# One 384-column f32 product for signal and taps, and one strided product for both masks of a score piece

## The chip, the core and the metric

The kernel runs on one core of a Trainium2 chip. The metric is the device time of one execution in microseconds, as the median of several runs; smaller is better. Five engines work beside each other on the core, each in its own fixed order and tied to the others by semaphores: TensorE (PE in the profile, its weight loads PEld), VectorE (DVE), ScalarE (ACT), GpSimd (POOL) and SyncE (SP), which issues most transfers here.

## The reference

Two independent blocks are computed, and their outputs stand side by side in the last axis.

```python
# A: sliding-window attention, S = 2048, D = 576, H = 32 heads of 18, window 256
qkv = (x @ wqkv).reshape(B, S, 3, H, Dh) ...
scores = einsum("bhqd,bhkd->bhqk", q, k) * Dh ** -0.5
mask = (i - j >= 0) & (i - j < 256)
o = softmax(where(mask, scores, -1e9)) @ v
a = o.reshape(B, S, D) @ wo
# B: S4 convolution, L = 2048, D = 576, N = 128 states
K[d, l] = Re sum_n C[d, n] * exp(dt[d] * A[d, n] * l) * dt[d] * B[d, n]
b = irfft(rfft(pad(u)) * rfft(pad(K)))[:L] + u * Dskip
return concatenate([a, b], axis=-1)
```

## The kernel before, in words

The convolution is a two-step Fourier transform. In the first half of the program the signal and the taps K go through a first transform step and are stored in DRAM as `gx` (signal) and `gk` (taps); the projections for q, k and v are made there too. The second half, stage "rest" of the plan, mixes the attention with the rest of the convolution. This stage is what the change touches.

**Spectra.** The second transform step is done in 24 executions (3 groups of 192 channels by 8 groups of frequencies). `conv_load(n)` (line 655) loads one tile `tx` [128, 4, 192] of the signal and one tile `tk` of the taps by two transfers of the SP queue (line 660); `cload` lets execution n be loaded once the products of n - 2 are issued. `spectra(n)` (line 665) then takes two slots of PSUM, `px` for the signal and `pk` for the taps, and does 16 f32 products into each (line 675): for i (real or imaginary result), q, s, r one product with 64 rows, 32 columns of weights and 192 columns of data. The 16 weight pieces are the same for signal and taps. Each f32 product appears in the trace as two matmul instructions and two weight loads. Three later steps follow: `first` copies the signal's spectrum `px` into SBUF as X on ACT (line 684); `second` multiplies X by the real and by the imaginary part of `pk` on DVE (lines 690 and 691); `third` makes the two sums on POOL (lines 696, 697) into Y. `inverse` (line 708) takes Y back by one step in one slot, with a copy on ACT (line 715), and `clast` (line 769) does the last step.

**Slots.** `slot()` (line 180) takes one tile [128, 2, 512] f32 of the pool `ring`, which has three such slots of two PSUM banks each. A slot can be written again when its last reader is done. Nearly all products of stage "rest" write to this ring: spectra two slots at a time, and one slot each for the inverse step, the last step, the row maxima (`smax1`, products at line 836, masks at line 844, DVE maxima at line 870), the transpose of the maxima (line 852), the scores and the output projection (line 178). Only P times V (line 956) has its own PSUM tile `po`.

**Scores.** For each of 16 sets (4 query chunks by 4 head groups) there are five pieces by two halves `pp`, 160 score pieces in all. `score1` (line 910) takes a slot, does four products for each key block of the piece (line 921), and then adds the mask as further products: the identity times a table `tm` that holds 0 or a very large negative number (line 930). `masks` lists the blocks of 64 columns in which a mask stands and joins neighbours to a run of 64 or 128 columns. Four of the five pieces have two such runs, apart from each other, the fifth has one; each run is four products of 64 rows by 64 columns of weights (two banks b by two row halves r, which lie on four different quarters of the array). So a set does 2 x 36 mask products. ACT then takes the exponential of the piece into P (line 936).

**Order.** Each engine works in the order in which the program issues its instructions, and this order is written out as a string of letters, `PLAN` (line 85): a letter is the next step of a stream (c spectra, a scores, s maxima, v P times V, d inverse, e last step, k loads of the convolution), and a letter with a digit is a posted later step of that stream (c1 is `first`, c2 `second`, c3 `third`; a1 is the exponential). The string is the same before and after the change.

Of the kernel before, what the change touches and what calls it, by code (L numbers as in the profile page):

```python
# [10 lines left out]
F32 = mybir.dt.float32  # L11
# [31 lines left out]
def constants():  # L43
    c = {}
    tau = 2 * np.pi
    l1, l2, f1, f2 = np.arange(64), np.arange(32), np.arange(64), np.arange(32)
    ph = -tau * np.outer(l1, f1 + 0.25) / 64
    m = np.stack([np.cos(ph), np.sin(ph)], 2).reshape(64, 128)
    wu = np.concatenate([m, m])
    wk = np.tile(m.reshape(32, 2, 128), (4, 1, 1))  # L50
    w2 = np.zeros((2, 2, 32, 8, 2, 2, 64))
    i1 = np.zeros((4, 32, 8, 2, 2, 64))
    for f in range(64):
        t, s, b = f // 8, f // 4 % 2, f % 4
# [12 lines left out]
    for nm, v in mult.items():  # L67
        t = np.zeros((3, GC, GC, len(v)))
        for g in range(GC):
            t[:, g, g] = v  # L70
        c[nm] = t.reshape(96, GC, len(v))
    big = -3e38
    p, x = np.arange(64)[:, None], np.arange(64)[None]
    sm = np.concatenate([np.where(x <= p, big, 0), np.where(x > p, big, 0)], 1)
    far, near, no = np.where(x >= p, big, 0), np.where(p > x, big, 0), np.zeros((64, 64))
    tm = np.concatenate([far, near, near, far, far, no], 1)
    c["c_sm"], c["c_tm"] = np.concatenate([sm, sm]), np.concatenate([tm, tm])
    c["c_if"] = np.eye(128)
# [52 lines left out]
class Kernel:  # L131
# [522 lines left out]

    def conv_load(self, n):
        nc, fs, (ch, t) = self.nc, self.p["fs"], divmod(n, 8)
        r = []
        for nm, g in (("tx", self.gx), ("tk", self.gk)):
            x = fs.tile([128, 4, 192], F32, name=nm)
            nc.sync.dma_start(x, g[8 * t:8 * t + 8, :, :, 192 * ch:192 * ch + 192]  # L660
                              .rearrange("(s r) a l j -> (r a l) s j", r=2))
            r.append(x)
        self.cl[n] = r

    def spectra(self, n):
        nc, tt, fy, t = self.nc, self.nc.vector.tensor_tensor, self.p["fy"], n % 8
        px, pk = self.slot(), self.slot()
        for x, ps in zip(self.cl.pop(n), (px, pk)):
            for i in range(2):
                for q in range(2):  # L670
                    for s in range(2):
                        for r in range(2):
                            b = 2 * q + (r ^ s)
                            o = (2 * s + q) * 64 + 32 * i
                            nc.tensor.matmul(ps[32 * b:32 * b + 32, s, 192 * i:192 * i + 192],  # L675
                                             self.w2[64 * r:64 * r + 64, t, o:o + 32],
                                             x[64 * r:64 * r + 64, 2 * s + q],
                                             start=(i == 0), stop=True, skip_group_check=True)
        v = lambda z: z[:, :, :384].rearrange("p s (i j) -> p s i j", i=2)
        sh = [128, 2, 2, 192]  # L680

        def first():
            X = fy.tile(sh, F32, name="X")
            nc.scalar.activation(X, v(px), AF.Copy)
            self.post("2", (X, pk), lambda: second(X))

        def second(X):
            t1 = fy.tile(sh, F32, name="t1")
            t2 = fy.tile(sh, F32, name="t2")
            tt(t1, X, v(pk)[:, :, 0:1].to_broadcast(sh), op=OP.mult)  # L690
            tt(t2, X, v(pk)[:, :, 1:2].to_broadcast(sh), op=OP.mult)  # L691
            self.post("3", (t1, t2), lambda: third(t1, t2))

        def third(t1, t2):
            Y = self.Y[n] = self.p["fs"].tile(sh, F32, name="Y")
            nc.gpsimd.tensor_tensor(Y[:, 0], t1[:, :, 0], t2[:, :, 1], op=OP.subtract)  # L696
            nc.gpsimd.tensor_tensor(Y[:, 1], t1[:, :, 1], t2[:, :, 0], op=OP.add)
            self.n["Y"] += 1
        self.post("1", (px, pk), first)

    def inverse(self, n):
        nc, (ch, t), Y = self.nc, divmod(n, 8), self.Y.pop(n)
# [36 lines left out]
    def cspec(self):  # L739
        self.spd = set()  # L740
        for n in range(24):
            yield "PE", lambda: self.cl[n], "ring", "ring", lambda: n in self.cl and self.n["Y"] >= n
            self.spectra(n)
            self.spd.add(n)

# [38 lines left out]
    def att_setup(self):  # L784
        nc, a, ap = self.nc, self.a, self.p["att"]
        self.idb = ap.tile([128, 64], BF, name="idb")
        self.sm = ap.tile([128, 128], BF, name="sm")
        self.tm = ap.tile([128, 384], BF, name="tm")
        self.idf = ap.tile([128, 128], F32, name="idf")
        for t, n in ((self.idb, "c_id"), (self.sm, "c_sm"), (self.tm, "c_tm"), (self.idf, "c_if")):  # L790
            nc.sync.dma_start(t, a[n])
        self.sets = []
        for b in range(3):
            d = {"Q": ap.tile([128, 4, CQ], F16, name="Q%d" % b), "K": ap.tile([128, 4, CK], F16, name="K%d" % b),
                 "V": ap.tile([128, 12 * 76 + 16], F32, name="V%d" % b)}
# [73 lines left out]
    def red(self, out, x):  # L869
# [2 lines left out]

    TB = [[(-1, 0), (4, 256)], [(-3, 0), (0, 128), (-4, 448)], [(7, 0), (1, 64), (6, 384)], [(-2, 0), (2, 192)],
          [(3, 0), (5, 320)]]
    MO = {(0,): 0, (1,): 64, (0, 1): 0, (1, 0): 128, (0, 0): 192, (1, 1): 64}

    def blocks(self, n, c):
        r = []
# [3 lines left out]
                r.append((rel, o, q0, q1 - q0))  # L882
        return r

    def masks(self, bl):
        m = {}
        for rel, o, q0, w in bl:
            if rel >= 0:
                m[o // 64] = 1
            if rel <= 3:  # L890
                m[(o + w) // 64 - 1] = 0
        ms, r = sorted(m.items()), []
        while ms:
            e = ms.pop(0)
            if ms and ms[0][0] == e[0] + 1:
                r.append((e[0], (e[1], ms.pop(0)[1])))
            else:
                r.append((e[0], (e[1],)))
        return r

    def scores(self):
        for i in range(16):
            for n in (2, 4, 0, 1, 3):
                bl = self.blocks(n, i // 4)
                self.Ps[i, n] = P = []
                for pp in range(2):
                    yield "PE", (self.sets[i % 3]["Q"],), "ring", lambda: self.maxed > i and len(self.Ps) < 3
                    self.score1(bl, self.sets[i % 3], pp, P)

    def score1(self, bl, d, pp, Ps):  # L910
        nc = self.nc
        ps = self.slot()
        lo = min(x[1] for x in bl)
# [1 line left out]
        for k, (rel, off, q0, w) in enumerate(bl):  # L915
            for b in range(2):
                for r in range(2):
# [3 lines left out]
                    nc.tensor.matmul(ps[z:z + 64, b, off:off + w], d["K"][rr, 2 * b + pp, kc:kc + 64],  # L921
                                     d["Q"][rr, 2 * b + pp, q0:q0 + w], start=(k == 0), stop=False,
                                     skip_group_check=True)
        for blk, kinds in self.masks(bl):
            w = 64 * len(kinds)
            for b in range(2):
                for r in range(2):
                    z = 64 * (r ^ b)
                    rr = slice(64 * r, 64 * r + 64)
                    nc.tensor.matmul(ps[z:z + 64, b, 64 * blk:64 * blk + w], self.idb[rr],  # L930
                                     self.tm[rr, self.MO[kinds]:self.MO[kinds] + w], start=False, stop=True,
                                     skip_group_check=True)

        def go():
            P = self.p["P"].tile([128, 2, 512], F32, name="P")
# [267 lines left out]
```

## Time and profile before

| | |
|---|---|
| median of 3 runs | 883.02 us (873.43 to 885.18) |
| profiled execution, its own time | 884.13 us |
| its span, first to last instruction | 882.3 us |
| mean granted TensorE clock | 0.922 |
| PE busy over the span | 724.2 us, 82% |
| DVE, ACT, POOL busy | 599.7, 522.7 and 378.0 us |

The profile comes from one execution and has several views: the page with busy times and costliest groups; the groups of instructions by line and shape (busy time together, mean ns of one, idle time before them and what ended it); the waits (who waited for whom: us in total, times, longest); the table by stretches; the timeline (start, length, engine, line, operation, output and inputs, shape, count). "Issue" as the end of a wait means that the trace shows nothing the engine waited for. A row such as "64*32 64x192 f32" is a product with 64 rows, 32 weight columns and 192 data columns. A matmul's end is modelled, so products on different parts of the array overlap in the rows, and the distance between starts says more than the length.

### The profile page before, as it was taken

What the parts mean: (1) busy time and instruction counts of PE and PEld (TensorE: products, weight loads), DVE (VectorE), ACT (ScalarE), POOL (GpSimd) and SP (SyncE); (2) the same over time, 40 slices, a digit from 0 to 9 for tenths busy, and PEclk for the clock granted to TensorE, in tenths of its full rate; (3) what the DMA queues carried; (4) which work ended last, traced back from release to release, by engine and by line L of the source; (5) the groups of instructions that cost most, each with busy time, mean ns of one, the idle gap of its engine ahead of it and who ended that gap; (6) DMA issues with size and microseconds to landing.
All of it is one profiled execution on the core that took longest, in us unless ns stands there. A gap on an engine that the chain in (4) does not pass through costs nothing.

```text
span 882.3 us, 32024 instructions
## 1 busy us (share of the span) xinstructions
PE 724.2 (82%) x14234; PEld 440.0 (50%) x14234; DVE 599.7 (68%) x798; ACT 522.7 (59%) x685; POOL 378.0 (43%) x295
## 2 busy tenths in 40 slices
PE   4565957998889789886888888887998987999977
PEld 2321523456446545454555554455555554567655
DVE  5855887887987787768657796575876767861010
ACT  3247676678777857671455566555766666676421
POOL 2256867766687655665015142221332042432020
PEclk9885969999999999996889999869999999999998
DMA  9795261546247745458549667637639573846743
GB/s 310 256 230 137 61 160 34 141 100 175 63 106 199 152 116 161 99 158 233 145 147 293 212 212 232 163 103 240 204 120 270 166 227 116 264 144 181 236 143 129
DMA packets 211051, 150.85 MB, mean 171 GB/s; under 512 B 102698, under 2 KB 191530, under 8 KB 210656
## 3 DMA queue, kind: packets, MB, share of 16 engines
q1 hardware_dynamic: 208896, 144.80, 58.5%
q0 software_dynamic: 2016, 3.99, 1.5%
q8 instruction: 112, 1.84, 0.9%
q14 instruction: 27, 0.22, 0.1%
HBM read 83.50 MB, written 65.11 MB: 168 GB/s over the span
## 4 chain that ended last, share of the span: by engine, by line
PE 46%; DVE 17%; ACT 12%; issue 10%; DMA 6%; SPq 4%; POOL 4%; ACTq 0%; DVEq 0%; POOLq 0%
PE pp L178 9%; PE po L956 7%; PE ring L178 6%; DVE m L870 5%; ACT P L936 4%; PE ring L708 4%; PE ring L921 4%; PE ring L836 3%; PE ring L675 3%; PE ring L575 2%; PE ring L453 2%; PE ring L769 2%; PE ring L465 2%; DMA K<-kz 1%; DVE m L552 1%
## 5 line engine op out<-in xcount | busy, mean ns | idle before, releaser
L870 DVE TENSOR_REDUCE m<-ring 128x2 f32<-128x640 f32 (+4 forms) x256 | 187.7, 779 | 66.6 <-PE ring L844 61.5
L936 ACT ACTIVATE P<-ring,esc 128x1024 f32<-128x1024 f32 (+2 forms) x160 | 166.8, 1060 | 102.3 <-PE ring L930 91.7
L546 POOL TENSOR_TENSOR m<-A,tr 128x1024 f32<-128x1024 f32 x72 | 144.0, 2017 | 79.2 <-DVE m L552 66.7
L956 PE MATMUL po<-P,V 64*32 64x320 f32 (+4 forms) x2816 | 105.7, 369 | 6.3 <-issue 6.3
L836 PE MATMUL ring<-K,Q 54*64 54x320 f16 (+4 forms) x1024 | 82.3, 322 | 26.5 <-DMA K<-kz 8.6
L696 POOL TENSOR_TENSOR Y<-t,t 128x384 f32<-128x384 f32 x24 | 24.0, 998 | 139.2 <-DVE t L691 133.3
L990 POOL TENSOR_TENSOR osb<-osb,T 128x1024 f32<-128x1024 f32 x16 | 37.8, 2362 | 100.6 <-DVE T L985 80.9
L921 PE MATMUL ring<-Q,K 55*64 55x320 f16 (+4 forms) x1408 | 67.7, 270 | 14.1 <-ACT P L936 3.4
L836 PEld LDWEIGHTS <-Q 54*64 54x64 f16 x1024 | 42.8, 109 | 71.7 <-issue 63.4
L998 POOL TENSOR_TENSOR oh<-osb,oh 128x1024 f16<-128x1024 f32 x16 | 34.1, 2130 | 73.5 <-ACT oh L994 73.5
L178 PE MATMUL pp<-xh,wh 128*128 128x512 f16 x180 | 48.6, 401 | 19.0 <-ACT vst L365 9.6
L178 PEld LDWEIGHTS <-wh 128*128 128x128 f16 x324 | 31.7, 101 | 57.1 <-issue 17.6
L844 PE MATMUL ring<-sm,idb 64*64 64x128 bf16 x896 | 56.9, 229 | 1.5 <-issue 1.5
L552 DVE TENSOR_TENSOR m<-m,m 128x1024 f32<-128x1024 f32 x36 | 53.3, 1480 | 4.8 <-POOL m L546 4.7
L956 PEld LDWEIGHTS po<-P,V 64*32 64x32 f32 x2816 | 39.1, 108 | 34.5 <-issue 25.0
L575 PE MATMUL ring<-Q,m 128*32 128x64 f32 x2304 | 42.6, 231 | 16.1 <-DVE m L552 13.4
L921 PEld LDWEIGHTS <-K 55*64 55x64 f16 x1408 | 33.8, 110 | 42.7 <-issue 34.0
L575 PEld LDWEIGHTS ring<-Q,m 128*32 128x32 f32 x2304 | 37.0, 117 | 29.8 <-issue 12.6
L178 PE MATMUL pp<-xh,wl 128*128 128x512 f16 x180 | 49.9, 412 | 0.0
L981 DVE STREAM_TRANSPOSE T<-osb 128x1024 f32<-128x1024 f32 x16 | 19.8, 1235 | 42.7 <-ACT osb L966 42.7
L930 PE MATMUL ring<-tm,idb 64*64 64x128 bf16 (+1 forms) x1152 | 44.9, 213 | 2.9 <-issue 2.9
L527 POOL TENSOR_TENSOR tr<-tr,mab 128x768 f32<-128x768 f32 x18 | 33.6, 1867 | 31.2 <-ACT tr L522 31.1
(162 smaller groups left out, 1570.2 us busy)
## 6 DMA issues: line engine op xcount, KB each, us to landing
gx<-ust SPq DMA_DIRECT2D x16, 576.0 KB
gk<-kst SPq DMA_DIRECT2D x18, 512.0 KB
tx<-gx SPq DMA_DIRECT2D x24, 384.0 KB
tk<-gk SPq DMA_DIRECT2D x24, 384.0 KB
h<-ho SPq DMA_DIRECT2D x48, 192.0 KB
hp<-h SPq DMA_DIRECT2D x12, 768.0 KB
Q<-qz SPq DMA_DIRECT2D x16, 512.0 KB
K<-kz SPq DMA_DIRECT2D x16, 512.0 KB
```

What stands on the lines that cost most here:

```text
L178: self.nc.tensor.matmul(ps, u, v, start=(i == 0), stop=(i == len(ops) - 1))
L546: tt(m[part], A[:, ch, a0:a0 + 8].unsqueeze(3).to_broadcast(sh), tr[:, ch, part, 0:8].unsqueeze(2).to_broadcast(sh), op=OP.mult)
L552: self.nc.vector.tensor_tensor(m[0], m[0], m[1], op=OP.add)
L575: nc.tensor.matmul(kp[32 * st:32 * st + 32, j, :], m[:, ch, 32 * term:32 * term + 32], Q[:, ch, term, :], start=(term == 0), stop=(term == ...
L836: nc.tensor.matmul(ps[z:z + 64, b, :n], d["Q"][rr, 2 * b + pp, 64 * qb:64 * qb + 64], d["K"][rr, 2 * b + pp, k0:k1], start=True, stop=Fals ...
L844: nc.tensor.matmul(out, self.idb[rr], self.sm[rr], start=False, stop=True, skip_group_check=True)
L870: self.nc.vector.tensor_reduce(out, x, axis=AX.X, op=OP.max)
L921: nc.tensor.matmul(ps[z:z + 64, b, off:off + w], d["K"][rr, 2 * b + pp, kc:kc + 64], d["Q"][rr, 2 * b + pp, q0:q0 + w], start=(k == 0), st ...
L930: nc.tensor.matmul(ps[z:z + 64, b, 64 * blk:64 * blk + w], self.idb[rr], self.tm[rr, self.MO[kinds]:self.MO[kinds] + w], start=False, stop ...
L936: nc.scalar.activation(P[:, :, lo:hi], ps[:, :, lo:hi], AF.Exp, scale=self.esc)
L956: nc.tensor.matmul(po[32 * p:32 * p + 32, z, q0:q0 + w], V[64 * z:64 * z + 64, kb * 76 + 19 * p:kb * 76 + 19 * p + 32], P[p % 2][64 * z:64 ...
L990: nc.gpsimd.tensor_tensor(osb, osb, rb, op=OP.mult)
```

## The change

Two things change, and the order of steps does not.

Spectra: signal and taps come into one tile `xk` [128, 4, 2, 192], by the same two transfers. One product takes the 2 x 192 = 384 columns of both for each weight piece, so there are 16 f32 products instead of 32. The two slots now hold the results by i instead of by signal and taps: `pi[i]` has the signal's spectrum in columns 0 to 191 and that of the taps in columns 192 to 383 of each bank. The copy X becomes two ACT instructions, one out of each slot, and each of the two DVE products reads the taps out of one slot.

Masks: the two runs of a piece are made in one product whose output has two runs, a fixed number of blocks apart. `MS` (sets 4 to 15) and `MF` (sets 0 to 3, which have no keys before them) give for each piece the place in the table, the first block, the width of a run and the step between the runs (0 for one run). Runs of unequal width are widened to 128 columns, with zeros (`no`) or where the table has what is needed. The table `tm` grows from 384 to 640 columns. A set now does 2 x 20 mask products.

```diff
-    tm = np.concatenate([far, near, near, far, far, no], 1)
+    tm = np.concatenate([near, near, far, near, far, far, near, no, far, near], 1)
...
-        r = []
-        for nm, g in (("tx", self.gx), ("tk", self.gk)):
-            x = fs.tile([128, 4, 192], F32, name=nm)
-            nc.sync.dma_start(x, g[8 * t:8 * t + 8, :, :, 192 * ch:192 * ch + 192]
+        x = self.cl[n] = fs.tile([128, 4, 2, 192], F32, name="xk")
+        for m, g in enumerate((self.gx, self.gk)):
+            nc.sync.dma_start(x[:, :, m], g[8 * t:8 * t + 8, :, :, 192 * ch:192 * ch + 192]
                               .rearrange("(s r) a l j -> (r a l) s j", r=2))
...
+        x, pi = self.cl.pop(n), (self.slot(), self.slot())
+        for i in range(2):
+            for q in range(2):
+                for s in range(2):
+                    for r in range(2):
+                        b = 2 * q + (r ^ s)
+                        o = (2 * s + q) * 64 + 32 * i
+                        nc.tensor.matmul(pi[i][32 * b:32 * b + 32, s, :384], self.w2[64 * r:64 * r + 64, t, o:o + 32],
+                                         x[64 * r:64 * r + 64, 2 * s + q].rearrange("p m j -> p (m j)"),
+                                         start=True, stop=True, skip_group_check=True)
...
-            nc.scalar.activation(X, v(px), AF.Copy)
-            self.post("2", (X, pk), lambda: second(X))
+            for i in range(2):
+                nc.scalar.activation(X[:, :, i], pi[i][:, :, :192], AF.Copy)
+            self.post("2", (X, *pi), lambda: second(X))
...
-            tt(t1, X, v(pk)[:, :, 0:1].to_broadcast(sh), op=OP.mult)
-            tt(t2, X, v(pk)[:, :, 1:2].to_broadcast(sh), op=OP.mult)
+            for i, tm in enumerate((t1, t2)):
+                tt(tm, X, pi[i][:, :, 192:384].unsqueeze(2).to_broadcast(sh), op=OP.mult)
...
-        self.tm = ap.tile([128, 384], BF, name="tm")
+        self.tm = ap.tile([128, 640], BF, name="tm")
...
-    MO = {(0,): 0, (1,): 64, (0, 1): 0, (1, 0): 128, (0, 0): 192, (1, 1): 64}
+    MS = [(2, 3, 128, 0), (2, 1, 128, 5), (0, 0, 128, 5), (5, 2, 128, 4), (6, 0, 128, 4)]
+    MF = [(1, 4, 64, 0), (1, 2, 64, 4), (0, 0, 128, 5), (1, 3, 64, 4), (6, 0, 128, 4)]
...
-        for blk, kinds in self.masks(bl):
-            w = 64 * len(kinds)
-            for b in range(2):
-                for r in range(2):
-                    z = 64 * (r ^ b)
-                    rr = slice(64 * r, 64 * r + 64)
-                    nc.tensor.matmul(ps[z:z + 64, b, 64 * blk:64 * blk + w], self.idb[rr],
-                                     self.tm[rr, self.MO[kinds]:self.MO[kinds] + w], start=False, stop=True,
-                                     skip_group_check=True)
+        at, blk, w, step = mask
+        n, flat = 2 if step else 1, ps.rearrange("p b x -> p (b x)")
+        for b in range(2):
+            for r in range(2):
+                z = 64 * (r ^ b)
+                rr = slice(64 * r, 64 * r + 64)
+                out = ps[z:z + 64, b, 64 * blk:64 * blk + w]
+                if step:
+                    o, e = 512 * b + 64 * blk, (64 * step - w) * b
+                    out = flat[z:z + 64, o - e:o - e + 128 * step].rearrange("p (t x) -> p t x", t=2)[:, :, e:e + w]
+                nc.tensor.matmul(out, self.idb[rr], self.tm[rr, 64 * at:64 * at + n * w], start=False, stop=True,
+                                 skip_group_check=True)
```

More of the change, by code (lines that the diff above doesn't have):

```diff
@@ L656, in conv_load @@
         nc, fs, (ch, t) = self.nc, self.p["fs"], divmod(n, 8)
-        r = []
-        for nm, g in (("tx", self.gx), ("tk", self.gk)):
-            x = fs.tile([128, 4, 192], F32, name=nm)
-            nc.sync.dma_start(x, g[8 * t:8 * t + 8, :, :, 192 * ch:192 * ch + 192]
+        x = self.cl[n] = fs.tile([128, 4, 2, 192], F32, name="xk")
+        for m, g in enumerate((self.gx, self.gk)):
+            nc.sync.dma_start(x[:, :, m], g[8 * t:8 * t + 8, :, :, 192 * ch:192 * ch + 192]
                               .rearrange("(s r) a l j -> (r a l) s j", r=2))
-            r.append(x)
-        self.cl[n] = r
     def spectra(self, n):
         nc, tt, fy, t = self.nc, self.nc.vector.tensor_tensor, self.p["fy"], n % 8
[L667 to L671, printed above, removed]
-                        for r in range(2):
[L673 to L679, printed above, removed]
+        x, pi = self.cl.pop(n), (self.slot(), self.slot())
[8 more added lines that the diff above has]
+                                         start=True, stop=True, skip_group_check=True)
         sh = [128, 2, 2, 192]
@@ L698, in third @@
             self.n["Y"] += 1
-        self.post("1", (px, pk), first)
+        self.post("1", pi, first)
     def inverse(self, n):
@@ L741, in cspec @@
         for n in range(24):
-            yield "PE", lambda: self.cl[n], "ring", "ring", lambda: n in self.cl and self.n["Y"] >= n
+            yield "PE", lambda: (self.cl[n],), "ring", "ring", lambda: n in self.cl and self.n["Y"] >= n
             self.spectra(n)
@@ L882, in blocks @@
                 r.append((rel, o, q0, q1 - q0))
[L883 to L898, printed above, removed]
         return r
@@ L907, in scores, with score1 @@
                     yield "PE", (self.sets[i % 3]["Q"],), "ring", lambda: self.maxed > i and len(self.Ps) < 3
-                    self.score1(bl, self.sets[i % 3], pp, P)
-    def score1(self, bl, d, pp, Ps):
+                    self.score1(bl, (self.MS if i >= 4 else self.MF)[n], self.sets[i % 3], pp, P)
+    def score1(self, bl, mask, d, pp, Ps):
         nc = self.nc
@@ L923, in score1 @@
                                      skip_group_check=True)
-        for blk, kinds in self.masks(bl):
-            w = 64 * len(kinds)
-            for b in range(2):
-                for r in range(2):
-                    z = 64 * (r ^ b)
-                    rr = slice(64 * r, 64 * r + 64)
-                    nc.tensor.matmul(ps[z:z + 64, b, 64 * blk:64 * blk + w], self.idb[rr],
-                                     self.tm[rr, self.MO[kinds]:self.MO[kinds] + w], start=False, stop=True,
-                                     skip_group_check=True)
+        at, blk, w, step = mask
[10 more added lines that the diff above has]
+                                 skip_group_check=True)
         def go():
```

## The prediction, made before the changed kernel was run

> **What bounds the kernel now.** I read the page first, then the table by stretches, then PE's waits in the stretch that the change touches, then the groups by shape, and last the timeline around single spectra.
>
> ```profile
> span 882.3 us, 32024 instructions
> PE 724.2 (82%) x14234; PEld 440.0 (50%) x14234; DVE 599.7 (68%) x798; ACT 522.7 (59%) x685; POOL 378.0 (43%) x295
> ...
> q8 instruction: 112, 1.84, 0.9%
> ```
>
> The execution took 884.13 us, 1.83 more than its span, and stands 1.1 above the median of 883.02. The sum below is made against 884.1. Spectra run from 447 to 792 us.
>
> ```profile
> 447.00:792.00 345.00, 297.79 (x8650) 182.21 (x8646) 250.60 (x327) 214.37 (x222) 104.48 (x73) 0.95 0.65 195
> ```
>
> There PE is busy 298 of 345 us (86%), DVE 251 (73%), ACT 214 (62%). Its idle 47 us end so, in the same stretch:
>
> ```profile
> PE po L956 <- issue: 6.3, 5, 4.1
> PE ring L836 <- ACT P L936: 5.9, 12, 0.9
> PE ring L675 <- issue: 4.8, 4, 1.8
> PE ring L836 <- DVE m L870: 3.3, 13, 0.4
> PE ring L921 <- DVE t L691: 2.9, 3, 1.4
> PE ring L930 <- issue: 2.9, 3, 1.6
> PE ring L708 <- issue: 2.8, 3, 1.8
> PE ring L921 <- issue: 2.4, 1, 2.4
> ...
> PE ring L836 <- issue: 1.8, 1, 1.8
> PE ring L844 <- issue: 1.2, 2, 0.8
> ```
>
> Two things stand out. Many waits are for a slot of the ring to come free (ACT or DVE as releaser of L836 and L921). And 22.2 us in 19 waits end with "issue", which means no semaphore. Two stretches from one such wait's end to the next one's:
>
> ```profile
> 543.39:549.06 5.67, 3.76 (x129) 2.49 (x128) 3.38 (x4) 2.12 (x2) 1.94 (x2) 1.00 0.90 284
> 608.23:614.34 6.11, 4.45 (x128) 3.15 (x128) 2.38 (x3) 2.66 (x3) 0.91 (x1) 1.00 0.72 243
> ```
>
> Each holds 128 products and 128 weight loads. The page has 112 transfers of instructions for 2 x 14234 PE instructions, 254 to a transfer. I take these waits as PE waiting for its next block of 256 instructions.
>
> **The products of spectra: no gain.** The change takes away 384 f32 products, 768 instruction pairs. Whether that is time depends on whether PE streams or issues. One execution, around 724 us:
>
> ```profile
> 724.39 0.86 PE L675 MATMUL ring<-tx,w 64*32 64x192 f32 x32
> 725.04 0.86 PE L675 MATMUL ring<-tk,w 64*32 64x192 f32 x32
> 725.36 0.81 ACT L684 ACTIVATE X<-ring 128x768 f32<-128x768 f32 x1
> 725.83 0.41 PE L921 MATMUL ring<-Q,K 55*64 55x320 f16 x8
> 726.07 0.26 PE L930 MATMUL ring<-tm,idb 64*64 64x64 bf16 x8
> 726.25 0.95 DVE L690 TENSOR_TENSOR t<-X,ring 128x768 f32<-128x768 f32 x1 [0.97 <-ACT X L684]
> 726.31 1.53 PE L708 MATMUL ring<-Y,i 32*64 32x192 f32 x32
> 726.38 1.11 ACT L936 ACTIVATE P<-ring,esc 128x1024 f32<-128x1024 f32 x1 [0.21 <-PE ring L930]
> 727.13 0.95 DVE L691 TENSOR_TENSOR t<-X,ring 128x768 f32<-128x768 f32 x1
> ```
>
> ```profile
> L956 PE MATMUL po<-P,V 64*32 64x320 f32 x1024 | 55.2, 463 | 0.8 <-issue 0.8
> L675 PE MATMUL ring<-tx,w 64*32 64x192 f32 x768 | 23.4, 343 | 1.3 <-ACT P L936 0.6 <-DMA tx<-gx 0.4 <-issue 0.4
> L844 PE MATMUL ring<-sm,idb 64*64 64x128 bf16 x896 | 56.9, 229 | 1.5 <-issue 1.5
> L930 PE MATMUL ring<-tm,idb 64*64 64x128 bf16 x768 | 37.2, 223 | 2.1 <-issue 2.1
> L930 PE MATMUL ring<-tm,idb 64*64 64x64 bf16 x384 | 18.1, 193 | 0.8 <-issue 0.8
> L507 ACT ACTIVATE mab<-ring 128x384 f32<-128x384 f32 x18 | 8.8, 491 | 3.6 <-PE ring L465 3.4
> L956 PE MATMUL po<-P,V 64*32 64x64 f32 x448 | 9.9, 227 | 4.1 <-issue 4.1
> ```
>
> From the first signal product to the first taps product pass 0.65 us for 32 instructions, 20 ns each. One such instruction streams far longer: between 64 and 320 columns the f32 product of the same 64 by 32 form grows from 227 to 463 ns, 0.92 ns a column, so 192 columns are 177 ns. Eight products (2 row halves by 4 column quarters) therefore run side by side, 177 / 8 = 22 ns each, which is the 20 ns seen. PE is at its streaming pace, and 384 columns in half as many products stream as long: 0 us. The bound below would be that busy time falls with the number of products; it is a rival.
>
> **The masks: no gain.** 512 of 1152 products go: in 128 of 160 pieces the second run's four are joined to the first's. Four products at once cost (223 - 193) / 64 = 0.47 ns a column for all of them, so the joined run adds 128 columns, 0.06 us, in which the second group's start stood before: the eight at 726.07 last 0.26 us from first start to last end, against about 0.2 for one group, so the second cost 0.04 to 0.06. I take 0. Bounds: -128 x 0.06 = -7.7 us if the added columns were free, +128 x 256 x 0.47 ns = +15.4 us if an output in two runs streamed at half pace. Against the latter stand two rows of 128 columns: L844, whose output is in two runs, 229 ns, and L930, in one run, 223.
>
> [...]
>
> **Fewer instruction blocks: -3.3 us.** 2 x 1280 PE instructions less are 10 blocks of 256. The stretch holds (8650 + 8646) / 256 = 68 blocks with 22.2 us of such waits, 0.33 a block. Bounds 0 and -22.2.
>
> **X in two copies: +1.4 us.** An ACT instruction of 384 columns out of the ring is 0.49 us (L507), two are 0.98 against 0.81: 0.17 x 24 = 4.1 us of ACT, idle there for 38%. I put a third on the path. Bounds 0 and 4.1.
>
> **Slots held longer: +10.5 us.** This is the term that decides. Before, the signal's slot is free when X is copied, and that copy starts when the first half of the products is done: 725.36, over at 726.17, and the inverse step takes the slot at 726.31. Afterwards each slot holds both signal and taps. The first copy can still start at 725.36, but the second needs the last product (725.90), so it runs from 726.01 to 726.50; the DVE product starts at 726.58 (0.33 later than before) and ends at 727.53, and only then is the first slot free, for PE at 727.67. The third slot offers no way out: its reader, the exponential at 726.38, ends at 727.49. So the inverse step starts 1.36 us later, and behind it on PE's queue wait P times V and the next scores, for which ACT and DVE wait.
>
> I read the same starts in all 24 executions: the shortfall is how much sooner than (last product's end + 1.77 us, or later where DVE is late) PE took that slot, less what a wait for L691 behind it would have taken anyway. The first and the last:
>
> ```profile
> 449.57 1.46 PE L675 MATMUL ring<-tk,w 64*32 64x192 f32 x32
> ...
> 451.50 0.83 PE L675 MATMUL ring<-tk,w 64*32 64x192 f32 x32
> ...
> 453.11 0.41 PE L921 MATMUL ring<-Q,K 55*64 55x320 f16 x8 [0.77 <-DVE t L691]
> ```
>
> ```profile
> 790.68 0.35 PE L675 MATMUL ring<-tk,w 64*32 64x192 f32 x2
> ...
> 792.28 0.79 PE L178 MATMUL ring<-woh,oh 128*128 128x288 f16 x5
> ```
>
> First: products end at 449.57 + 1.46 = 451.03, the second execution's slot would be free at 452.80 instead of 451.50, 1.3 late, of which the wait of 0.77 takes most: 0.5. Last: end 791.03, free at 792.80 against 792.28: 0.5. The 24 together make 18.1 us, from 0 to 1.6 each. Of this 86% (PE's busy share) falls on the path, 15.6. PE's block fetch goes on in such a pause: 19 of 68 blocks end in a wait, so 19 / 68 of 18.1 = 5.1 come back. Left: +10.5. Bounds: 0 (PE reaches the ring later anyway), and 24 x 1.3 = 31 with nothing absorbed.
>
> **At no cost.** The two transfers of a load both wait for all products of two executions before, 0.65 us later on SP for the first; covered by the next execution being some 14 us off (345 / 24), and +0.65 each without that cover. What is late next is the load itself, which PE waited for only 0.4 us (in the L675 row). The DVE products keep their 768 elements, 0.95 us. DVE stands 0.33 us longer before the first of them, with the row maxima queued behind and PE's ring behind those; its 94 idle us cover that, 24 x 0.33 = 7.9 us if not. The mask table grows by 128 x 256 x 2 bytes, 0.3 us at the stretch's 195 GB/s, once, behind other loads.
>
> **Sum:** 0 + 0 - 3.3 + 1.4 + 10.5 = +8.6, so 884.1 + 8.6 = 892.7, said as 893 us.
>
> **Rivals.** (1) *Issue is the bound, much faster.* If PE's busy time went with the number of products, spectra would give back what the signal's row holds, 23.4, and masks 512 / 1152 of 55.3 (37.2 + 18.1), 24.6: 836 us. A weaker form, in which all "issue" waits go: 862. Against the strong form stands the 20 ns pace; for the weak one, that the waits hang on instruction blocks. Chance 0.12 for both.
>
> [...]
>
> (2) *The hold costs nothing*, since PE finds P times V to do or takes the third slot: -3.3 alone, 881. For it: several executions have 1 us of P times V before the next slot is asked for. Against: the exponential that frees the third slot ends no sooner. Chance 0.17.
>
> (3) *The hold is paid in full, slower.* With 18.1 all on the path, the 7.9 on DVE, 4.1 on ACT and -3.3: 911 us. It decides from a hold of about 1 us per execution that nothing absorbs (24 us - 3.3 is past 2%). For it: 12 + 13 waits of L836 show that the ring is short already. Chance 0.19.
>
> (4) *Output in two runs at half pace:* 8.6 + 15.4, 908 us. Chance 0.04.
>
> **How the numbers follow.** Forecast 0.48, rivals 0.12, 0.17, 0.19, 0.04. The forecast's own range is 878 to 900. The range of 8 in 10 is 866 to 911: it leaves out most of (1) and half of (3). A measurement here tells about 2% (17.7 us) from no change; within it lie the forecast and (2), 0.65; faster 0.12; slower (3) and (4), 0.23.
>
> **What would show it.** PE with 12954 instructions and about 102 instruction transfers. L675 with 768 instructions of 64x384 at 480 to 520 ns, and again 1.3 us from an execution's first start to its last group's end of streaming. L930 with 640 products and unchanged time per piece. X as 48 copies near 0.49 us. New waits of PE for the DVE products of `second`, 10 to 20 us together, where L921 and L691 had 2.9. If those waits are absent, the central term is wrong; if PE's time in L675 halves, the streaming argument is; if L930 gets longer per column, the strided output is what I mispriced.

## The result and the profile after

The change takes 876.62 us (22 runs, 872.16 to 884.81) against 882.43 for the kernel before (22 runs, 873.43 to 890.9): ratio 0.9943 with a 95% interval of 0.9924 to 0.9962. It is 5 us faster; the forecast was 10 us slower (893). A second set of runs gave 0.9939 (0.9905 to 0.9973). The ratios here and below leave out executions that stand over 1.5% above the fastest of their kernel, so a ratio can differ from that of the medians beside it. The direction was wrong: the time is 16 us under the forecast, inside the range of 8 in 10 (866 to 911) and just outside the forecast's own (878 to 900).

The profiled execution of the change took 875.76 us. Its page:

```profile
span 874.0 us, 29447 instructions
PE 719.8 (82%) x12954; PEld 417.3 (48%) x12954; DVE 601.3 (69%) x798; ACT 526.9 (60%) x709; POOL 378.1 (43%) x295
...
q8 instruction: 101, 1.65, 0.8%
```

The counts are those of the change: 1280 PE products less, 11 instruction transfers less (112 before), 24 ACT instructions more. The groups by shape:

```profile
L671 PE MATMUL ring<-xk,w 64*32 64x384 f32 x768 | 39.9, 524 | 5.5 <-DVE m L865 2.5 <-DMA xk<-gk 1.7 <-ACT P L919 0.8
L914 PE MATMUL ring<-tm,idb 64*64 64x256 bf16 x448 | 34.0, 283 | 0.1
L914 PE MATMUL ring<-tm,idb 64*64 64x128 bf16 x160 | 9.7, 222 | 0.0
L679 ACT ACTIVATE X<-ring 128x384 f32<-128x384 f32 x48 | 23.4, 490 | 10.8 <-PE ring L671 8.2 <-DVE t L686 1.1 <-ACT osb L949 0.2
```

L671 is the product of spectra (L675 before), L914 the masks (L930), L679 the copies of X (L684). Next PE's waits while spectra run; columns are the total, the number of waits and the longest:

```profile
PE ring L703 <- DVE t L686: 6.7, 6, 1.6
PE ring L901 <- DVE t L686: 5.6, 8, 1.2
PE ring L831 <- ACT P L919: 5.5, 12, 0.9
PE po L939 <- issue: 4.7, 5, 1.4
PE ring L831 <- DVE m L865: 4.3, 17, 0.4
PE ring L831 <- DVE t L686: 3.0, 4, 1.5
...
PE ring L764 <- DVE t L686: 1.2, 2, 0.6
...
PE ring L671 <- DVE t L686: 0.4, 1, 0.4
PE ring L703 <- issue: 0.4, 1, 0.4
...
PE ring L831 <- issue: 0.3, 1, 0.3
```

Two things changed places. Waits for the DVE products of spectra (L686, before L690 and L691) rose from 3.9 us to 16.9. Waits that end with "issue", which the prediction reads as waits for the next block of instructions, fell from 22.2 us to 5.4 (8.0 in a second execution of the change). The trace before bears that reading out: from one of the 19 to the next there are 126 to 128 products, or a multiple of about 127.5 (255, 383, 510, 765, 1020). What is left is seen when the stage is taken from the first to the last product of spectra, before and after:

```profile
448.30:791.00 342.70, 295.49 (x8588) 180.78 (x8579) 249.66 (x325) 213.88 (x221) 103.48 (x73) 0.95 0.65 194
```

```profile
446.20:782.40 336.20, 288.26 (x7386) 158.35 (x7378) 248.97 (x325) 217.46 (x244) 103.98 (x73) 0.96 0.66 197
```

PE's idle time is 342.70 - 295.49 = 47.2 us before and 47.9 after (48.6 and 50.6 in a second execution of each). The hold of the slots has put about as much in as the blocks have given back, and PE's busy time is 7 us shorter. Single executions stray from their kernel's median (those profiled of the hold alone by -11.6, of spectra alone by +6.1 and of the split scores by +6.0), so below, times carry the verdicts, and waits are given for two executions where there are two.

### The profile page after: what moved, and what is told of

It reads as the page before. It is cut to its first block, busy times and chain, and to the rows that moved or that the text cites. A ratio compares the mean times of both kernels' runs of the same rounds, so it can differ in the third digit from the quotient of the medians.

```text
span 874.0 us, 29447 instructions
## 1 busy us (share of the span) xinstructions
PE 719.8 (82%) x12954; PEld 417.3 (48%) x12954; DVE 601.3 (69%) x798; ACT 526.9 (60%) x709; POOL 378.1 (43%) x295
## 5 line engine op out<-in xcount | busy, mean ns | idle before, releaser
L939 PE MATMUL po<-P,V 64*32 64x320 f32 (+4 forms) x2816 | 101.6, 364 | 4.7 <-issue 4.7
L691 POOL TENSOR_TENSOR Y<-t,t 128x384 f32<-128x384 f32 x24 | 24.0, 1002 | 138.9 <-DVE t L686 129.9
L981 POOL TENSOR_TENSOR oh<-osb,oh 128x1024 f16<-128x1024 f32 x16 | 34.1, 2134 | 68.6 <-ACT oh L977 68.5
L178 PE MATMUL pp<-xh,wh 128*128 128x512 f16 x180 | 48.4, 400 | 18.6 <-ACT vst L365 9.2
L686 DVE TENSOR_TENSOR t<-X,ring 128x768 f32<-128x768 f32 x48 | 43.4, 945 | 25.5 <-ACT X L679 18.3
L575 PEld LDWEIGHTS ring<-Q,m 128*32 128x32 f32 x2304 | 37.0, 117 | 29.6 <-issue 11.9
L178 PE MATMUL pp<-xh,wl 128*128 128x512 f16 x180 | 50.6, 417 | 0.0
```

The costliest lines, as they stand in the source:

```text
L178: self.nc.tensor.matmul(ps, u, v, start=(i == 0), stop=(i == len(ops) - 1))
L575: nc.tensor.matmul(kp[32 * st:32 * st + 32, j, :], m[:, ch, 32 * term:32 * term + 32], Q[:, ch, term, :], start=(term == 0), stop=(term == ...
L686: tt(tm, X, pi[i][:, :, 192:384].unsqueeze(2).to_broadcast(sh), op=OP.mult)
L939: nc.tensor.matmul(po[32 * p:32 * p + 32, z, q0:q0 + w], V[64 * z:64 * z + 64, kb * 76 + 19 * p:kb * 76 + 19 * p + 32], P[p % 2][64 * z:64 ...
```

## The experiments

Three theories. **T1:** fewer instruction blocks give back over 1 us each, and the hold costs about the 10 us forecast. **T2:** the hold costs nothing and the gain lies in the masks themselves, as shorter work of PE. **T3:** PE's pauses for a slot are time in which blocks arrive, so the hold is cheap as long as blocks are late. Prices below are differences of ratios times 882.

### The parts alone

*Masks alone, twice:* before.py with the new table, `MS`, `MF` and the strided product, spectra untouched.

> The joined masks alone, spectra as before: 512 pairs of PE instructions less (4 blocks of 256), no slot held longer. Theory 1 (fewer instruction blocks give back some 1.2 to 1.7 us each, a slot held longer costs some 10): 5 to 7 us faster, issue waits of PE in the stage clearly under 22. Theory 2 (the hold costs nothing and the whole gain comes from the masks): about 6 us faster, with no fewer issue waits but PE busy time down. Theory 3 (PE's waits for held slots are what hides the block fetch): about 1 us faster, issue waits near 22.

> The kernel before with the joined masks alone, once more, beside the change on the same chip. T1 (the products of spectra save 6 blocks worth some 7 us, the hold costs about 10): 1 to 5 us faster than the change or equal. T2 (the gain is the masks alone): equal within 2 us. If spectra gain by themselves: the change is faster by over 2 us.

Measured 877.25 us, 0.9945 (0.9908 to 0.9982), and 876.76, 0.9938 (0.9901 to 0.9975): 5 us faster. The change itself ran beside the second of them:

> The changed kernel once more, on the chip of the run with the early slot and of the masks alone: all theories expect 875 to 879 us.

It took 878.09. Masks alone give the whole gain; the edit of spectra adds nothing to it that shows beside these intervals. Waits for blocks in the second run of the masks:

```profile
PE ring L675 <- issue: 7.8, 7, 2.6
...
PE ring L906 <- issue: 4.0, 2, 2.8
PE po L944 <- issue: 3.9, 3, 2.1
...
PE ring L708 <- issue: 1.8, 1, 1.8
...
PE ring L844 <- issue: 0.9, 1, 0.9
```

With one of 0.2 they are 18.6 us, and 17.0 in the first run, against 22.2 in each of two executions of the kernel before. The second of these comes from one more run of it:

> The kernel before once more, for a second profile of it: near 882 us. All theories expect its waits that end with issue to be 18 to 26 us in the stage. If the busy time of PE in the stage is again 295 us, the 7 us that the change takes from it are the change's doing; if it is 287 to 289 us as in the profiles of the edits, they are the spread of single executions, and T1 stands alone.

It took 880.13 us (0.9996, 0.9962 to 1.0031), with PE busy 292.4 us in the stage: 3 of the 7 us were the spread of executions.

*Spectra alone, twice:* the change with the masks as before.

```
-        n, flat = 2 if step else 1, ps.rearrange("p b x -> p (b x)")
...
+        for blk, kinds in self.masks(bl):
+            w = 64 * len(kinds)
```

> The products of 384 columns alone, masks as before: 768 pairs less (6 blocks), slots held longer. Theory 1: hold +10, blocks -8 to -10, so within 2 us of before, waits for the DVE products near 13 us above before. Theory 2: no change within 1 us. Theory 3: 2 to 6 us faster, since the waits for slots take the place of the issue waits and the blocks are fewer as well.

> The products of spectra in 384 columns with the masks as before, once more, since its profiled execution stood 6 us over the median of its runs. T1 with T3 (6 blocks fewer give back some 0.5 us each beside a hold that pauses already fill): 880 to 883 us, 2 to 4 under the hold alone, waits that end with issue at 5 to 12 us. T2: 881 to 883 and issue waits that do not answer to the number of products.

Measured 881.27 us, 0.9975 (0.9934 to 1.0016), and 884.2, 1.001 (0.9975 to 1.0045): no difference from before. Waits for blocks stayed at 18.1 and 17.8 us, where T1 and T3 had expected 5 to 12 of the second.

*The hold alone, twice:* slots by row half and X in two copies, but signal and taps in products of 192 columns each, and the masks as before. No instruction of PE is saved.

```
-        for i in range(2):
+        for i, m in ((0, 0), (0, 1), (1, 0), (1, 1)):
...
-                        nc.tensor.matmul(pi[i][32 * b:32 * b + 32, s, :384], self.w2[64 * r:64 * r + 64, t, o:o + 32],
-                                         x[64 * r:64 * r + 64, 2 * s + q].rearrange("p m j -> p (m j)"),
-                                         start=True, stop=True, skip_group_check=True)
+                        nc.tensor.matmul(pi[i][32 * b:32 * b + 32, s, 192 * m:192 * m + 192],
+                                         self.w2[64 * r:64 * r + 64, t, o:o + 32], x[64 * r:64 * r + 64, 2 * s + q, m],
+                                         start=(m == 0), stop=True, skip_group_check=True)
```

> Slots filled by i as in the change, X in two copies, but each weight piece loaded twice for 192 columns, and the masks of before: as many PE instructions as before, only the hold is new. Theory 1: 8 to 12 us slower, issue waits near 22. Theory 2: same as before within 1 us. Theory 3: 0 to 4 us slower, issue waits down to under 12 with the instruction count unchanged.

> The hold alone (slots by row half, X in two copies, products and masks in their old number) once more, since its profiled execution stood 11 us under the median of its runs. T1 (the hold has a price of about 10 us that nothing gives back): 890 us and more. T2 (the hold costs nothing): 881 to 883, like the kernel before. T3 (pauses for a slot give block fetch time, so that about two thirds of the hold come back): 884 to 887, with PE's waits for DVE products near 17 to 20 us and its waits that end with issue down from 22.2 to 8 to 14 us.

Measured 884.56 us, 1.0011 (0.9964 to 1.0057), and 888.54, 1.0048 (1.0012 to 1.0083). The hold has a price, 1 and 4 us by the ratios, 3 and 7 by the medians, and in the second run it is clear of noise. So T2's "nothing" falls, and so does the forecast's 11.9 for it (10.5 and 1.4 for X): the upper ends of the two intervals are 5.0 and 7.3 us. Its waits in the second run:

```profile
PE ring L703 <- DVE t L686: 7.5, 7, 1.6
PE ring L916 <- DVE t L686: 6.3, 8, 1.3
...
PE ring L831 <- issue: 4.3, 2, 4.1
PE ring L831 <- DVE t L686: 3.2, 5, 1.5
PE ring L916 <- issue: 3.2, 2, 1.9
PE ring L671 <- issue: 2.8, 4, 1.3
PE po L951 <- issue: 2.8, 3, 2.0
PE ring L925 <- issue: 2.6, 2, 2.2
...
PE ring L703 <- issue: 1.6, 1, 1.6
```

Slot waits for L686 are 18.4 us here (19.9 in the first run). Issue waits are 17.3, and 11.2 in the first: with every instruction still there, 5 to 11 us of them went. That is the way T3 says, but its numbers for the second run (884 to 887 us, 8 to 14 us of issue waits) were missed.

The parts add up: masks -5.2 (mean of both ratios), hold +2.6, and the step from the hold to spectra alone, which takes 768 products out, 0.9993 - 1.0030 = -3.3. Sum -5.9; the change measured -5.0 and -5.4. The masks and the hold have an uncertainty of some 2.5 us each and the -3.3 one of 3.5, so the single prices are rough.

### Is it the number of instructions?

The change with each score product of 320 columns in two of 160: the columns and the result stay, 512 PE products and as many weight loads (4 blocks) come back.

```
+            h = w // 2 if w == 320 else w
+            parts += [(rel, off + a, q0 + a, h, k == 0 and a == 0) for a in range(0, w, h)]
```

> The changed kernel with each score product of 320 columns given as two of 160 columns: 512 more PE products and weight loads, 4 more instruction blocks of 256, no column more to stream, the result unchanged. T1 (fewer instruction blocks give back 1.2 to 1.7 us each): 4 blocks cost 5 to 7 us, so 881 to 884 us beside 876.6 for the change, with the waits of PE that end with issue up from 5.4 to about 10 us or more in the stage. T2 (the gain is in the joined masks themselves, not in their count): 876 to 877 us. T3 (the block fetch is hidden in PE's waits for slots): between the two, 877 to 880, waits that end with issue up by at most 2 us.

Measured 883.2 us, 0.9988 (0.9951 to 1.0025): 4 us by the ratios (with an uncertainty of almost 4) and 6.6 by the medians over the change, as T1 expected; T3's 877 to 880 was missed. Its waits for blocks:

```profile
PE po L943 <- issue: 4.8, 5, 1.9
PE ring L905 <- issue: 3.4, 2, 2.1
PE ring L703 <- issue: 3.2, 2, 2.0
...
PE ring L839 <- issue: 2.0, 1, 2.0
...
PE ring L764 <- issue: 1.2, 1, 1.2
```

With two smaller groups 15.6 us, 10 and 8 more than in the two executions of the change; slot waits are as in the change. A whole piece (score products and masks, where nothing stalls and the clock is full) of 192 and 320 columns takes some 400 to 415 ns on average before, in the change and with the split: no difference in streaming shows. So it is the count, at 1.0 to 1.7 us a block. T2 falls.

### With fewer transfers

Kernels with part of the stage's transfers left out (loads of spectra from the third on, which use the first two tiles again, stores of h from the ninth on, loads of hp from the third on). The stage moves 39.8 MB instead of 66.6 in the profiles; the 31 MB of the expectations are those of the whole program. What these kernels compute as the convolution is not the reference's.

```
+        if n > 1:
+            self.cl[n] = self.fix[n % 2]
+            return
...
-            for s in range(2):
+            for s in range(2 if n < 8 else 0):
```

> The kernel before with fewer transfers in the stage: the spectra loads of all executions from the third on are left out (the first two executions' tiles are used again), the h stores from the ninth on and the hp loads from the third on are left out too, some 31 of 67 MB of the stage, so the convolution that it computes is not the reference's. T1 and T3 (blocks of instructions come late because other transfers stand before them): PE's waits that end with issue fall from 22.2 us to at most 8 in the stage, and the time falls by at least as much, to 850 to 870 us. If instruction blocks come late for another reason, the issue waits stay near 20 us and the time falls only by what PE waited for loads, under 5 us.

> The kernel before with fewer transfers once more (the same loads and stores of the convolution left out, so its convolution is not the reference's), since five runs spread over 15 us. If the hold costs 5 us or more once transfers are few: 858 to 865 us, 4 or more under the light change (868.7). If not: 867 to 870.

> The changed kernel with the same transfers left out as in the kernel before with fewer transfers; the convolution is not the reference's. T1 and T3: with no late blocks to save, what is left of the change is its hold of slots, so it is no faster than the light kernel before, and up to 10 us slower (the 15.6 of the prediction before what the block fetch gave back, less what is absorbed). T2: it is about 5 us faster than the light kernel before, as with the full transfers.

> The kernel that takes only the hold (signal and taps of one row half in one slot, products of 192 columns in their old number) together with the joined masks of the change, if any of its parts, as in the run of the hold alone, and with the same transfers left out; the convolution is not the reference's. T1 and T3: with block fetch out of the way the hold shows its own price against the light kernel without it, 5 to 15 us. T2 (the hold costs nothing): within 2 us of it.

The kernel before took 866.08 and 864.75 us with them left out (0.9756, 0.9686 to 0.9826, and 0.979, 0.9737 to 0.9842), the change 868.7 (0.9864, 0.9817 to 0.9911), the hold alone 872.78 (0.9899, 0.9853 to 0.9945). Against the mean of the first two, the change is now *slower*, by 3 us in the medians and 8 by the ratios, and the hold costs 7 to 11. The light kernel before still waits for blocks:

```profile
PE po L963 <- issue: 7.5, 7, 2.4
...
PE ring L843 <- issue: 2.5, 2, 2.3
...
PE ring L678 <- issue: 0.9, 1, 0.9
```

10.9 us, and 13.1 in the first run, more than the 8 at most that T1 and T3 allowed: about half of the waits went with the transfers. The light hold has 7.8 us. The light change has 0.7 in all; its list, down to 0.3 us, has no such row:

```profile
PE ring L706 <- DVE t L689: 7.9, 7, 1.6
PE ring L838 <- DVE m L872: 6.0, 17, 2.0
PE ring L908 <- DVE t L689: 5.8, 8, 1.2
PE ring L838 <- ACT P L926: 5.8, 13, 0.9
PE ring L674 <- DVE m L872: 4.0, 1, 4.0
PE ring L838 <- DVE t L689: 3.0, 4, 1.5
```

With all transfers and with fewer, the hold takes up a part of the block waits: 22.2 us become 17.3 and 11.2, and 13.1 and 10.9 become 7.8. In the times T3 has less behind it. By the ratios the hold costs 2.6 us with all transfers and 11 with fewer; by the medians it is 3 and 7 against 7 and 8, which the spread of the runs could make. So T1 stands for the count, and T3 for the way the waits go; that the hold is dearer where fewer blocks are late is likely, not shown.

### Two ways to shorten the hold

*Both halves copied to SBUF:* ACT copies 768 columns out of each slot (signal and taps), DVE multiplies from there, and the slots are free after the copies.

```
-                nc.scalar.activation(X[:, :, i], pi[i][:, :, :192], AF.Copy)
-            self.post("2", (X, *pi), lambda: second(X))
+                nc.scalar.activation(X[:, i], pi[i][:, :, :384], AF.Copy)
+            self.post("2", (X,), lambda: second(X))
...
-                tt(tm, X, pi[i][:, :, 192:384].unsqueeze(2).to_broadcast(sh), op=OP.mult)
+                tt(tm, X[:, :, :, :192].rearrange("p i s j -> p s i j"),
+                   X[:, i, :, 192:384].unsqueeze(2).to_broadcast(sh), op=OP.mult)
```

> The change, with the hold taken away: ACT copies signal and taps of each slot together into SBUF (0.81 us a slot, 0.64 us more per execution), and the DVE products read SBUF alone, so a slot is free after its copy. Theory 1: 8 to 12 us faster than the change, less up to 5 for ACT, so 864 to 872; waits of PE for the DVE products gone. Theory 2: not faster than the change (876), rather 3 slower by ACT. Theory 3: at most 3 us faster than the change, since issue waits come back where the slot waits go.

Measured 882.86 us, 1.0032 (0.9999 to 1.0066): no gain over before, 6 us over the change by the medians.

```profile
PE ring L832 <- DVE m L866: 19.8, 22, 3.4
PE ring L671 <- DVE m L866: 5.3, 1, 5.3
PE po L940 <- issue: 4.8, 5, 1.4
```

```profile
L686 DVE TENSOR_TENSOR t<-X 128x768 f32<-128x768 f32 x47 | 57.7, 1268 | 29.9 <-ACT X L679 22.0 <-issue 5.7 <-POOL Y L693 2.1
```

No wait for L686 is left, but DVE's product takes 1268 ns on average, against 945 with one input in the slot, and the row maxima (L866) behind it on DVE now hold PE up. The pause moved. The mean mixes two kinds: 40 of the 48 products take 917 to 1036 ns, and eight take 1776 to 3120, each of them while POOL is at a product of its own in SBUF (six of the 40 met one as well). Two products of DVE, one of them such a long one:

```profile
513.98 3.98 DVE L686 TENSOR_TENSOR t<-X 128x768 f32<-128x768 f32 x2
...
514.14 3.01 POOL L974 TENSOR_TENSOR osb<-osb,T 128x1024 f32<-128x1024 f32 x1 [9.35 <-DVE T L969]
```

In the change, with one input in the slot, all 48 take 916 to 955 ns, whether POOL is busy or not.

*Slots by signal half:* slot s takes the 16 products of signal half s, and one DVE product per slot reads both of its taps.

```
-        for i in range(2):
+        for s in range(2):
...
-                        nc.tensor.matmul(pi[i][32 * b:32 * b + 32, s, :384], self.w2[64 * r:64 * r + 64, t, o:o + 32],
+                        nc.tensor.matmul(pi[s][32 * b:32 * b + 32, i, :384], self.w2[64 * r:64 * r + 64, t, o:o + 32],
...
-            for i, tm in enumerate((t1, t2)):
-                tt(tm, X, pi[i][:, :, 192:384].unsqueeze(2).to_broadcast(sh), op=OP.mult)
+            for s in range(2):
+                tt(tm[:, s], X[s].unsqueeze(1).to_broadcast(sh), pi[s][:, :, 192:384].unsqueeze(2).to_broadcast(sh), op=OP.mult)
```

> The changed kernel with the two slots of an execution of spectra divided by the signal half s instead of the row half i: the first slot is complete after the first 16 products, its half of X is copied at once, and one DVE product of 768 elements reads both of its taps, so it comes free after about 0.65 + 0.11 + 0.49 + 0.08 + 0.95 + 0.14 = 2.4 us instead of 3.1 from the first product; number and size of all instructions stay, the result is unchanged. If the hold of the first slot has a price beside the blocks (T1), PE's waits for the DVE products of spectra fall from 16.8 us by 24 x 0.65 = 15.6 at most, some 6 to 10 with what is late for other reasons, of which part comes back as waits for instruction blocks: 868 to 874 us, 2 to 8 under the change. If the hold costs nothing because the waits only stand in for block waits (T2 and T3), 875 to 878, with waits that end with issue up by as much as the slot waits fall.

> The change with the slots divided by signal half (first slot free 0.65 us earlier) and with the same transfers left out; the convolution is not the reference's. T3 (slot waits are cheap only while they cover block fetch): with no block waits left to cover, the shorter hold shows in full, 3 to 6 us under the light change (868.7), where it was 1.5 with all transfers. If the hold costs nothing in itself: 868 to 869.

Measured 876.6 us, 0.9928 (0.9896 to 0.9961), where the change had 878.09 and 0.9939 on the same chip; slot waits fell from 17.0 to 12.3 us, and issue waits (5.2 us) did not take their place. T1's 868 to 874 was missed. With fewer transfers 869.78, 0.9835 (0.979 to 0.9881), against 868.7 and 0.9864, while slot waits fell from 18.8 to 13.6 us. Medians and ratios contradict each other in sign there, so neither is a difference. T3 had expected 3 to 6 us with fewer transfers; that was not seen. One possible reason shows in the trace: the median execution of spectra in which nothing stalls lasts 1.68 and 1.63 us from first start to last end in this order and 1.52 in the change's, which by estimate takes 24 x 0.11 to 24 x 0.16, some 3 to 4 us, back. No version here beats the change for certain.

## Why the prediction was wrong, step by step

**Products of spectra, 0 us: right.** L671 has 768 products at 524 ns (480 to 520 said, so a little over). The median execution in which nothing stalls lasts 1.53 us before and 1.52 after, from the first start to the last end; the 1.3 of the prediction leaves out the last group's end, with which its own rows make 1.51. In the sum over all 24, PE's time in them at full clock (start to next start, less idle) fell from 36.6 to 34.1 us, mostly where a block came late inside one.

**Masks, 0 us: right.** The same sum is 24.7 us before and 25.5 after. The output in two runs is not slower (the half pace of rival 4, +15.4 us, shows in no run), and no shorter either (T2). Masks give the gain all the same, by T1 through the blocks.

**Fewer instruction blocks, -3.3 us: wrong.** The step that failed is "22.2 us of such waits, 0.33 a block". It shares the waits out over all 68 blocks, late or not, and takes away the share of ten. Measured: 4 blocks less are -5.2 us (1.3 each), 4 blocks more +4.0 to +6.6, 6 blocks less in spectra -3.3 (0.55 each, hardly clear of noise); ten together some -8.5.

**Slots held longer, +10.5: waits right, price wrong.** This is the larger failure. The waits came where and as large as said (10 to 20 us for L686, measured 16.9 and 17.0). One execution of the change, for the chain that the prediction wrote down:

```profile
713.46 1.50 PE L671 MATMUL ring<-xk,w 64*32 64x384 f32 x32
...
714.42 0.49 ACT L679 ACTIVATE X<-ring 128x384 f32<-128x384 f32 x1
...
715.06 0.49 ACT L679 ACTIVATE X<-ring 128x384 f32<-128x384 f32 x1 [0.15 <-PE ring L671]
...
715.66 1.82 DVE L686 TENSOR_TENSOR t<-X,ring 128x768 f32<-128x768 f32 x2 [2.23 <-ACT X L679]
...
716.67 1.53 PE L703 MATMUL ring<-Y,i 32*64 32x192 f32 x32 [1.26 <-DVE t L686]
```

Products end at 713.46 + 1.50 = 714.96, and the inverse step gets the slot at 716.67, 1.71 later (1.77 said), after an idle of 1.26. What failed is the next sentence: "19 of 68 blocks end in a wait, so 19 / 68 of 18.1 = 5.1 come back". In the hold alone 5 to 11 us of block waits went, and the price was 1 to 4 us by the ratios (3 to 7 by the medians), with X's copies in it, instead of 11.9. X's +1.4 was not measured by itself.

**The common fault.** Both failed terms treat a late block as a matter of chance, at one rate for all blocks, whatever work stands before it. Counting blocks of 128 products from one issue wait to the next in the kernel before: the 18 that end in a wait had 4.5 us of work on average, the 40 that don't 5.2, and from the start of a block to the start of the one that came late passed 4.3 us at least and 9.4 at most. There is no sharp threshold, since 13 of the 40 others were followed by the next block within 4.2 us. It reads as a race between PE's work on one block and the coming of the next, which takes a varying time. Taking ten blocks out makes the rest last 336.2 / 58 = 5.8 us instead of 342.7 / 67 = 5.1, and each pause for a slot makes its block longer too. Both would shrink the late part of *every* block, and that would explain why ten blocks and 13 us of pauses took 16.8 and 14.2 us in the two executions, not the 8.4 forecast. It doesn't explain spectra alone, where six blocks less and the same pauses left 18.1 and 17.8. So this account is argued, not shown. That the fetch starts with the block before is inferred from these times; no transfer of a single block was followed.

Most blocks came with no wait of their own: in this stage 19 of 67 came late, with 22.2 us of waits, and the other 48 show none.

**What stays open.** In the profiles the exchange of waits leaves PE's idle time as it was, and the gain stands in busy time, 294 us (mean of two executions before) against 288 (two of the change). Half of that is time at half clock, 32.0 against 27.7 us of the stage, 3 us of busy time. The masks alone look alike, with 47.0 and 43.8 us idle, 289.0 and 288.1 busy, and 20.5 and 17.1 at half clock. But half clock varied from 10.6 to 37.5 us among the profiles here, and the mean clock of all runs was the same for the masks alone (0.925 and 0.924) as in the sets of before (0.923 to 0.926). For the change it was 0.928 and 0.931. Over the 117 runs of before, 0.001 more of mean clock goes with about 0.3 us less time; by that estimate 1 to 3 us of the change's 5 may go with the clock, and nothing of the masks' 5. I can't say that late blocks cause it.

Of the rivals, "the hold costs nothing" (881) came nearest in time, with both of its terms off: the hold does cost, and blocks give back more than 3.3. The weak form of the first ("all issue waits go") was nearly right about those waits and left out what took their place.

## What to carry to other kernels

Where a profile shows an engine waiting with no semaphore behind it at every 128th product, price an instruction by the late blocks (here 22.2 us / 19 = 1.2 us a block), not by the mean over all blocks. That came near for the masks (1.3) and the split scores (1.0 to 1.7), less so for spectra (0.55). In such a stage fewer, wider instructions can pay even where their streaming is unchanged (the masks here: 24.7 us of PE before, 25.5 after, and 5 us less time), and a new wait on the same engine can cost much less than its length: here some 15 us of new slot waits cost 1 to 7, and block waits fell meanwhile.

## What the runs showed of the hardware

- A product whose output lies in two runs of 128 columns cost PE about as much as two products: the masks of the stage took 24.7 us before and 25.5 after.
- A DVE product of 768 f32 elements took 916 to 955 ns with one input in PSUM, whether POOL was busy or not. With both inputs in SBUF 40 of 48 took 917 to 1036 ns, and eight took 1776 to 3120, all beside a product of POOL in SBUF.
- Leaving out 27 of the stage's 67 MB of transfers took about half of the block waits away (22.2 to 13.1 and 10.9 us), not all.
- Granted clock fell to half in stretches of about 3.4 us or multiples of it (3.41, 6.83, 13.65 us in the trace before).
